# Two transformer layers on one core: the query projection put in place by DMAs instead of two masked products, and layer two's last 256 rows in one chunk instead of two

## The chip, the cores and the metric

One core of a Trainium2 chip runs the whole program: TensorE (PE, with its weight loads PEld), VectorE (DVE), ScalarE (ACT), GpSimd (POOL) and SyncE (SP, which here only issues DMAs), around an on-chip memory (SBUF) and the accumulators of TensorE (PSUM, eight banks of 128 partitions by 512 float32). The metric is device time in microseconds of one execution; the time of a kernel is the median of its runs.

## The reference, cut to what matters

The sequence has 2048 rows of 512 numbers in bfloat16. An attention layer A and a feed-forward layer B are applied twice, with the same weights both times. There are 32 heads of 16 numbers each, and the hidden width of B is 1792.

```python
def A(x, wqkv, wo):                       # 32 heads, 16 wide
    qkv = (x @ wqkv).reshape(B, S, 3, 32, 16).transpose(2, 0, 3, 1, 4)
    q, k, v = qkv
    p = softmax(einsum("bhqd,bhkd->bhqk", q, k) * 16 ** -0.5)
    return einsum("bhqk,bhkd->bhqd", p, v).transpose(0, 2, 1, 3).reshape(B, S, 512) @ wo
def Bff(x, w1, w2):
    return maximum(x @ w1, 0) @ w2
x = x + A(layernorm(x)); x = x + Bff(layernorm(x))
x = x + A(layernorm(x)); x = x + Bff(layernorm(x))
```

The exponentials are the mass of it: 2 layers x 32 heads x 2048 x 2048 = 268 million, in the kernel's layout 4096 blocks of 128 keys by 512 queries.

## The kernel before, in words

**Layout.** K and Q are kept transposed, 16 numbers of a head on 16 partitions. A *strip* T (there are four, T = 0 to 3) is 128 columns of the K or Q weights, so 128 partitions with eight heads; they sit as four row groups g of 32 partitions, each with two heads e = 0 and 1. A score matmul takes the 32 partitions of one group (line 1411); to keep the head e alone, the Q operand `qbuf[n % 2][:, e]` has zeros on the partitions of the other head. `q_masked` (line 680) makes both copies in one DVE instruction that reads the PSUM bank twice and multiplies it by a mask of 0 and the softmax scale: 128x1024 results.

**Runs and segments.** The queries are cut into chunks of rows, `chunks` (line 460): four of 512 rows in layer one (l = 0); in layer two (l = 1) two of 512, then three of 256 (lines 461 and 462), then two of 128 (lines 464 and 465); `LAST = 6` is the last chunk. A *run* is a layer, a chunk, a strip and a range of key blocks; its two *segments* are the heads e = 0 and 1 of the strip, and one segment's sums fill the one bank `ps_o`. Where a run takes only some of the key blocks (lines 862 to 871), its sums are *stored* in buffers of the layer that is not in use (`acc`, `acc0`, lines 145 to 151), and the later run adds them to its own: line 910 writes the sum of both to one of three buffers `u`.

**The loop** (line 1282) goes slot by slot, 1366 slots in all. A slot takes three blocks of scores (PSUM tiles `ps_s`, two of three banks each, used in turn). ACT exponentiates the three banks in one instruction of 128x1536 (line 1420), or only two of them, 128x1024, and the third goes to DVE, which makes the exponential of it with integer arithmetic and a cubic: line 1105 (`lin`) for each block, and for every two such blocks, a *pair*, lines 1146, 1157, 1146 and 1161 on 128x1024 (and line 1158 for the few pairs without prepared values). A block of DVE costs TensorE three products with V (`lin`, `step`, `cube`) instead of one.

**What sets the order.** The kernel writes out the order of every engine by hand: a planner keeps clocks for PE, DVE and ACT (`now_pe`, `now_dve`, `exp_end`) with costs for each instruction and lags for DMAs (line 80: `C_LAG`, `R_LAG`, `U_LAG`), and chooses what to issue next. Projections, output products and the feed-forward layer are *groups* of matmuls into the one bank `ps_f`, put between the slots (`mm_group`, line 428); each is evacuated by DVE. Line 1309 decides, by the DVE work already queued, whether a slot gives a block to DVE. An engine then executes in that order, each instruction waiting for its semaphores; so does the SP queue.

**Finishing a segment** (`finish_segment`, line 882): DVE copies `ps_o` to `u` (line 912; line 910 with stored sums), an SP DMA moves the row of sums to `c` (line 917), DVE takes the reciprocal (line 939), an SP DMA puts it back (line 940), a POOL DMA spreads it over 32 partitions into `r` (line 942; a `quick` segment uses a DVE shuffle, line 952), and DVE multiplies (line 928). Three sets of `u`, `r`, `c` go in turn; before the fourth is begun, the multiplication of the first is put into the order (lines 899 and 900).

**The start** (lines 182 to 201, 1172 to 1239): x and weights are loaded on the SP and ACT queues; K and Q weights 512 columns at a time (`load_w`, line 179); `w2`, 1.8 MB, is issued at line 195, then four slices of `w1` (line 719), then the transposes of the normalized rows of the next chunks (line 573), all on SP. POOL fills constants (lines 199 and 201) and has the small arithmetic of layernorm (lines 492 to 500). The normalized rows are in four buffers `xn` (line 157).

**The end** (from line 1454): after the last exponential, the last chunk's output product, layernorm, feed-forward layer and store, with lines 1473 (matmuls), 1483, 1513, 1525, 1527 and 1540; also one row block of the second part of the chunk before (`half_part`, line 1495).

Of the kernel before, what the change touches and what calls it, by code (L numbers as in the profile page):

```python
# [12 lines left out]
BF16 = mybir.dt.bfloat16  # L13
# [12 lines left out]
def kernel(  # L26
# [52 lines left out]
    FLOOR = 0.56  # L79
    C_LAG, R_LAG, U_LAG = 3600.0, 13000.0, 3000.0  # L80
    VLAG = 1
    X_ISSUE, X_LAG = 1400.0, 7500.0
    RSTD_LAG = 4000.0
    AHEAD = (8.0, 8.0)
    LATE = 0.0
# [22 lines left out]
    qmask = masks[:, 2:4]  # L108
    wqkv = sb([P, NDC, 3 * D], BF16, "wqkv")
    wo = sb([P, NDC, D], BF16, "wo")  # L110
# [67 lines left out]

    def load_w(engine, a):
        engine.dma_start(out=wqkv[:, :, a : a + D], in_=wq_src[:, :, a : a + D])  # L180

# [6 lines left out]
    nc.scalar.activation(out=warm[:], in_=warm[:], func=ACTF.Exp)  # L188
    load_w(nc.sync, D)
    load_w(nc.scalar, 0)  # L190
    load_x(nc.sync, (4, 5, 6, 7))
    load_w(nc.scalar, 2 * D)
    load_x(nc.sync, range(8, NTT))
    nc.sync.dma_start(out=wo[:], in_=A_wo[:, :].rearrange("(c p) f -> p c f", p=P))
    nc.sync.dma_start(out=w2[:], in_=B_w2[:, :].rearrange("(c p) f -> p c f", p=P))

    make_identity(nc, ident[:])
    for kb in range(NKB):
        nc.gpsimd.memset(vaug[0][kb][:, :, DH : DH + 2], 1.0)
    for kb in range(NKB - TPC):  # L200
        nc.gpsimd.memset(vaug[1][kb][:, :, DH : DH + 2], 1.0)


    wide = [True]
# [256 lines left out]
    HALF = TPC // 2  # L461
    for n in range(3):
        chunks[1, 2 + n] = (2 * TPC + n * HALF, HALF)
    chunks[1, 5] = (3 * TPC + HALF, 1)
    chunks[1, 6] = (3 * TPC + HALF + 1, 1)
    LAST = 6

# [46 lines left out]
    def ln_root(tag, rows):  # L514
# [11 lines left out]
        stt(out=y, in0=t1, scalar=1.5, in1=y, op0=ALU.add, op1=ALU.mult)  # L526

    def ln_apply(tag, tt, i):
        n = ln_n(tag)
        nc.vector.tensor_scalar(  # L530
            out=xnbuf[i][:], in0=x_t[tt][:],
            scalar1=mv[n][:, i, 0:1], scalar2=ya_[n][:, i : i + 1],
            op0=ALU.subtract, op1=ALU.mult,
        )

    def ln_transpose(tag, i, b=None, at_bank=None):
        pt = bank().bitcast(BF16) if b is None else b
        for c in range(NDC):
            ins = nc.tensor.transpose(
                pt[:, c * P : (c + 1) * P], xnbuf[i][:, c * P : (c + 1) * P], ident[:]  # L540
            )
            if wide[0]:
                uses(ins, in_bank[0] if b is None else at_bank)
        mark(("xT", tag, i), "pe")
        return pt[:, 0 : NDC * P].rearrange("p (c f) -> p c f", c=NDC)
# [4 lines left out]
    def ln_rows(tag, tt, n, i):  # L550
# [10 lines left out]
        if i == n - 1:  # L561

            def rstd():
                ln_seed(tag, n)
                mark(("rs", tag, 3), lag=RSTD_LAG)

            task(0, rstd, [("rs", tag, 3)], each(n, "st", tag) + old)
            def apply(k):
                ln_apply(tag, tt + k, k)
                if not by_dma(tag):  # L570
                    return
                _, l, j = tag
                nc.sync.dma_start_transpose(
                    out=xnT[j][:, :, k * P : (k + 1) * P], in_=xnbuf[k][:]
                )
                sp_free[0] = max(sp_free[0], now_dve[0]) + X_ISSUE
                lag = sp_free[0] + X_LAG - now_dve[0]
                mark(("xT", tag, k), lag=lag)
                mark(("xnT", tag, k), lag=lag)

            for k in range(n):
                task(
                    325, lambda k=k: apply(k),
                    [("xn", tag, k)] + [("xT", tag, k), ("xnT", tag, k)] * by_dma(tag),
                    [("xT", prev, k)] * (k < rows_of_prev) + [("rs", tag, 3)],
                )

    def ln_groups(tag, dst, at_column, n, war):
        groups = []
        for i in range(0, n, 2):  # L590
            hold = {}

            def piece(k, i=i, hold=hold):
                if not k % 2:
                    hold["b"] = bank()
                half = hold["b"].bitcast(BF16)[:, k % 2 * D : (k % 2 + 1) * D]
                ln_transpose(tag, k, half)
                m = min(2, n - i)
                if k - i < m - 1:
                    return  # L600
                pt = hold["b"].bitcast(BF16)[:, 0 : m * D].rearrange(
                    "p (i c f) -> p c i f", i=m, c=NDC
                )

                def fin():
                    a = at_column + i * P
                    nc.vector.tensor_copy(
                        out=dst[:, :, a : a + m * P].rearrange("p c (i f) -> p c i f", i=m), in_=pt
                    )
                    for of in range(i, k + 1):  # L610
                        mark(("xnT", tag, of))

                put_evac(609 if m == 2 else 342, fin)

            groups.append(
                group(
                    [(1.3, lambda k=k, piece=piece: piece(k)) for k in range(i, min(i + 2, n))],
                    [(key, tag, k) for key in ("xT", "xnT") for k in range(i, min(i + 2, n))],
                    [("xn", tag, k) for k in range(i, min(i + 2, n))] + war,
                )  # L620
# [6 lines left out]
    def k_mms(T, j):  # L627
        return [(wqkv[:, c, D + T * P : D + (T + 1) * P], xnT[j][:, c, :]) for c in range(NDC)]

# [10 lines left out]
    def v_mms(kb):  # L640
        j, i = divmod(kb, TPC)
        return [
            (xnT[j][:, c, i * P : (i + 1) * P], wqkv[:, c, 2 * D : 3 * D]) for c in range(NDC)
        ]
# [29 lines left out]
    def q_mms(l, j, T):  # L674
        xj, a, w = columns(l, j)
        return [
            (wqkv[:, c, T * P : (T + 1) * P], xnT[xj][:, c, a : a + w]) for c in range(NDC)
        ]
# [8 lines left out]
    def q_group(n, l, j, T):  # L687
        xj, _, w = columns(l, j)
        cost = 90 + 2.09 * w

        def fin(b):
            q_masked(n, b, w)
            mark(("q", n))

# [20 lines left out]
    def load_w1(n):  # L715

        if n < (NQS + LAST - 1) * NF + NW1:
            ft = n % NF
# [7 lines left out]

    def per_group(w):
        return min(QS // w, 2)

    def h_group(l, j, ft, war):  # L730
        n = (l * NQS + j) * NF + ft
        xj, a, w = columns(l, j)

        number = per_group(w)
        fts = range(ft, ft + number)
# [14 lines left out]
        def after():  # L750
            for f in range(number):
                load_w1(n + f + NW1)
            for _ in range(min(2, len(w1_to_load))):
                home, of = w1_to_load.popleft()
                mark(("kept", of), "pe", 6000.0)
                nc.sync.dma_start(
# [5 lines left out]
            [  # L762
                (
                    (w1_last[ft + f] if (l, j) == (1, LAST - 1) else w1buf[(n + f) % NW1])[:, c, :],
                    xnT[xj][:, c, a : a + w],
                )
                for f in range(number) for c in range(NDC)
            ],
            fin, made_here,
            each(w // P, "xnT", ("ln2", l, j)) + war + [  # L770
                ("kept", ft + f) if (l, j) == (1, LAST - 1) and ft + f >= NW1 else ("w1", n + f)
                for f in range(number)
            ],
            after=after, wide_by=w, sums=number, cost=77 + 1.045 * number * w,
        )

# [19 lines left out]
    def before(l, j):  # L796
# [3 lines left out]
        if not j:  # L800
            return 0, NQS - 1
        first, rows = chunks[l, j]
        return max(
            (l, b) for b in range(j)
            if chunks[l, b][0] % TPC <= first % TPC < chunks[l, b][0] % TPC + chunks[l, b][1]
        )
# [3 lines left out]
    def rest_of_chunk(l, j):  # L810

        if (l, j) == (1, LAST - 2):
            for ft in range(NF):
                home = (
                    w1buf[((l * NQS + LAST - 1) * NF + ft) % NW1] if ft < NW1
                    else (kt01 + kt2)[(ft - NW1) // 2][:, ft % 2, :].rearrange(
# [12 lines left out]
        )  # L829
        gs = [h_group(l, j, ft, war_h) for ft in range(0, NF, per_group(w))]  # L830
        gs += [z_group(l, j, i) for i in range((l, j) == (1, LAST - 1), n)]
# [47 lines left out]

    sums_wait = [0]  # L880

    def finish_segment(sg, last):
# [16 lines left out]
        if n >= NU:  # L899
            run_until(("m", n - NU))  # L900
        u, r, c = ubuf[n % NU], rbuf[n % NU], cbuf[n % NU]
        lane = DH if e == 0 else DH - 1
# [32 lines left out]
        ended[l, j] = ended.get((l, j), 0) + 1  # L935
        quick = ended[l, j] == NT or sg["load"] is not None and sg["busy"] or width == P

# [39 lines left out]
        elif sg is segs[-2]:  # L977
            task(1560 * width // P, direct_all, ots + [("m", n)], war + [("u", n)])
        else:
# [203 lines left out]
    for e in range(2):  # L1183
# [3 lines left out]
            op=ALU.add, axis=mybir.AxisListType.XY,  # L1187
        )
        nc.vector.tensor_scalar(
            out=qmask[:, e : e + 1], in0=mask[e], scalar1=SCALE * LOG2E * UNIT, scalar2=None,  # L1190
            op0=ALU.mult,
# [382 lines left out]
```

## Time and profile before

| what | value |
|---|---|
| time, median of 3 runs | 1583.8 us (1582.8 to 1585.81) |
| the profiled execution's own time | 1582.8 us |
| its span, first to last instruction | 1580.9 us |
| granted TensorE clock | 0.999 |
| first exponential begins | 14.98 us |
| last exponential ends | 1558.87 us |
| ACT busy with exponentials | 1539.8 us |
| matmul records of the scores (L1411) | 6699 |
| DMA moved | 44.98 MB, mean 28 GB/s |

The page gives, for each engine, the time in which it was busy, and the chain of work that ended last, followed back from the end. Groups of instructions are named by source line, engine, operation, and what they write and read. A group's mean duration reaches from start to end, and neighbouring instructions of one engine overlap a little, so that count times mean is over the busy time. The timeline gives start, duration, engine and line, and in brackets how long the engine had been idle and what released it. SPq is the SP queue's issuing of DMAs.

### The profile page before, as it was taken

The numbers are of one execution on the slowest core, as the hardware profiler recorded it, in microseconds if no ns is written. First come the engines' busy times: TensorE is split into PE (matmuls) and PEld (weight loads), VectorE is DVE, ScalarE is ACT, GpSimd is POOL, SyncE is SP. The second block draws the span as 40 slices with busy tenths as digits, with TensorE's granted clock in tenths as the row PEclk, the third lists the DMA queues.
The fourth block names the chain that finished last, engine by engine and source line by source line (L and its number), as shares of the span: only waits on it lengthen the run. The fifth ranks groups of instructions, "written<-read, shape, count | busy, mean of one in ns | idle before, by whom it ended". The sixth has DMA issues, their size and how long they took to land.

```text
span 1580.9 us, 48353 instructions
## 1 busy us (share of the span) xinstructions
PE 1431.2 (91%) x21308; PEld 551.6 (35%) x21311; DVE 1502.9 (95%) x2947; ACT 1549.1 (98%) x1387; POOL 96.6 (6%) x243
## 2 busy tenths in 40 slices
PE   8888889998999989999899998888999999999898
PEld 3222223232332222333223222222334444545665
DVE  7889999999999999999899999999999999999895
ACT  6999999999999999999999999999999999999995
POOL 2000001001010010000100000001001000010000
PEclk9999999999999999999999999999999999999999
DMA  6001100111012120120101000000210211212030
GB/s 194 15 2 24 21 9 16 42 29 24 6 19 43 25 29 7 22 52 12 26 2 27 22 2 1 2 4 9 59 21 17 43 34 27 60 25 59 18 75 16
DMA packets 130145, 44.98 MB, mean 28 GB/s; under 512 B 119280, under 2 KB 127216, under 8 KB 129936
## 3 DMA queue, kind: packets, MB, share of 16 engines
q1 hardware_dynamic: 116864, 29.37, 8.8%
q0 software_dynamic: 11728, 11.23, 4.0%
q8 instruction: 166, 2.72, 0.7%
q10 hardware_dynamic: 1344, 1.31, 0.3%
q14 instruction: 43, 0.35, 0.1%
HBM read 24.38 MB, written 2.10 MB: 17 GB/s over the span
## 4 chain that ended last, share of the span: by engine, by line
ACT 78%; PE 11%; DVE 8%; issue 2%; DMA 1%; SPq 0%; ACTq 0%; DVEq 0%
ACT e L1420 78%; PE ps_s L1411 4%; PE ps_f L446 3%; PE ps_o L998 3%; DVE lin L1105 2%; DVE step L1146 1%; DVE cube L1157 1%; DVE cube L1161 1%; PE ps_s L1473 1%; DVE ht L744 0%; DMA wqkv<-in_A_wqkv_dram 0%; DVE q L681 0%; DVE ot L928 0%; DMA w<-in_B_w_dram 0%; DVE u L912 0%
## 5 line engine op out<-in xcount | busy, mean ns | idle before, releaser
L1420 ACT ACTIVATE e<-ps_s 128x1024 bf16<-128x1024 f32 (+1 forms) x1366 | 1539.8, 1357 | 6.1 <-PE ps_s L1411 5.3
L1411 PE MATMUL ps_s<-q,ktp 32*128 32x512 bf16 (+2 forms) x6699 | 608.3, 324 | 112.8 <-ACT e L1420 102.1
L998 PE MATMUL ps_o<-e,vaug 128*32 128x512 bf16 (+2 forms) x4682 | 495.3, 328 | 8.4 <-DVE u L912 2.7
L1105 DVE TENSOR_SCALAR lin<-ps_s 128x512 int16<-128x512 f32 x696 | 475.9, 686 | 23.4 <-PE ps_s L1411 17.3
L1411 PEld LDWEIGHTS <-ktp 32*128 32x128 bf16 x6699 | 209.0, 91 | 560.6 <-issue 411.0
L998 PEld LDWEIGHTS <-vaug 128*32 128x32 bf16 x6644 | 175.8, 94 | 290.2 <-issue 265.3
L1146 DVE TENSOR_SCALAR step<-lin 128x1024 int16<-128x1024 int16 x696 | 274.2, 420 | 2.1 <-PE ps_o L998 1.2
L1157 DVE TENSOR_TENSOR cube<-step 128x1024 f16<-128x1024 bf16 x348 | 236.5, 684 | 1.7 <-PE ps_f L446 0.5
L1161 DVE TENSOR_TENSOR cube<-cube,lin 128x1024 bf16<-128x1024 f16 x348 | 236.6, 681 | 0.0
L998 PE MATMUL ps_o<-step,vaug 128*32 128x512 bf16 (+2 forms) x950 | 159.5, 327 | 0.0
L446 PE MATMUL ps_f<-w,ht 128*32 128x512 bf16 x1680 | 152.2, 381 | 1.2 <-DVE ht L744 0.5
L446 PE MATMUL ps_f<-xnT,w 128*32 128x512 bf16 (+2 forms) x2080 | 148.2, 341 | 4.9 <-DVE ht L744 3.1
L998 PE MATMUL ps_o<-cube,vthird 128*32 128x512 bf16 (+2 forms) x888 | 143.4, 326 | 0.0
L998 PE MATMUL ps_o<-lin,vaug 128*32 128x512 bf16 (+2 forms) x950 | 125.0, 326 | 6.2 <-DVE u L912 3.7
L446 PE MATMUL ps_f<-xnT,wqkv 128*32 128x512 bf16 (+2 forms) x1376 | 107.9, 351 | 5.2 <-DVE ht L744 1.1
L942 POOL DMA_DIRECT2D r<-u x53 | 39.0, 736 | 1077.6 <-DVE lin L1105 438.0
L446 PE MATMUL ps_f<-wo,ot 128*32 128x512 bf16 x992 | 88.0, 381 | 1.3 <-DVE x L705 1.0
L744 DVE TENSOR_SCALAR ht<-ps_f 128x512 bf16<-128x512 f32 (+1 forms) x107 | 73.0, 682 | 2.9 <-PE ps_f L446 2.3
L446 PEld LDWEIGHTS <-w 128*32 128x32 bf16 x2080 | 59.2, 96 | 34.6 <-issue 17.6
L681 DVE TENSOR_TENSOR q<-ps_f,masks 128x1024 bf16<-128x1024 f32 (+2 forms) x55 | 54.3, 987 | 7.8 <-PE ps_f L446 5.9
L446 PEld LDWEIGHTS <-ht 128*32 128x32 bf16 x1680 | 48.7, 96 | 28.7 <-issue 13.1
L998 PEld LDWEIGHTS <-vthird 128*32 128x32 bf16 x888 | 44.0, 95 | 28.5 <-issue 23.4
(106 smaller groups left out, 610.7 us busy)
## 6 DMA issues: line engine op xcount, KB each, us to landing
w<-in_B_w_dram SPq DMA_DIRECT2D x130, 128.0 KB
r<-u POOLq DMA_DIRECT2D x32, 256.0 KB, 7.4
r<-u POOLq DMA_DIRECT2D x21, 128.0 KB, 4.8
out_dram<-x SPq DMA_DIRECT2D x16, 128.0 KB
x<-in_A_x_dram SPq DMA_DIRECT2D x14, 128.0 KB
w<-in_B_w_dram SPq DMA_DIRECT2D x1, 1792.0 KB
ktp<-in_B_w_dram SPq DMA_DIRECT2D x10, 128.0 KB
wqkv<-in_A_wqkv_dram ACTq DMA_DIRECT2D x2, 512.0 KB
```

The source lines that it names most:

```text
L446: nc.tensor.matmul(out[cols], lhsT[:, cols], rhs, start=i % k == 0, stop=i % k == k - 1, tile_position=(0, 32 * g), skip_group_check=True,)
L681: return nc.vector.tensor_mul(out=qbuf[n % 2][:, :, 0:w], in0=b.rearrange("p (e q) -> p e q", e=1).to_broadcast((P, 2, w)), in1=qmask.rear ...
L744: nc.vector.tensor_scalar(out=out, in0=sums, scalar1=0.0, scalar2=None, op0=ALU.max)
L942: nc.gpsimd.dma_start(out=r[:, 0:width], in_=bass.AP(tensor=sums.tensor, offset=sums.offset, ap=[list(sums.ap[0]), [0, 32], [1, width]],),)
L998: nc.tensor.matmul(ps_o[32 * g : 32 * g + 32, 0 : sg["w"]], values[:, 4 * sg["T"] + g, 2 * e : 2 * e + 32], rhs, start=g not in sg["begun" ...
L1105: first = nc.vector.tensor_scalar(out=lin[which][:, half * QS : (half + 1) * QS], in0=src, scalar1=EXP_BIAS, scalar2=0.0, op0=ALU.add, op1 ...
L1146: nc.vector.tensor_scalar(out=stair, in0=line, scalar1=keep, scalar2=put, op0=ALU.bitwise_and, op1=ALU.bitwise_or,)
L1157: (609, lambda: nc.vector.tensor_mul(out=power, in0=mantissa, in1=mantissa)),
L1161: (609, lambda: nc.vector.tensor_mul(out=power.bitcast(BF16), in0=power, in1=line.bitcast(BF16))),
L1411: nc.tensor.matmul(b[:, a : a + sg["w"]], kt[32 * g : 32 * g + 32, kc : kc + P], qbuf[sg["n"] % 2][32 * g : 32 * g + 32, sg["e"], 0 : sg[" ...
L1420: ex = nc.scalar.activation(out=eb[:, 0 : place[m]], in_=b[:, 0 : place[m]], func=ACTF.Exp, scale=1.0 / (LOG2E * UNIT),)
L1473: uses(nc.tensor.matmul(out, lhsT, rhs, start=first, stop=last), b, needs=needs)
```

## The change

**Weights.** The K and Q weights get buffers of their own, `wkq`, in which the two heads of a group are interleaved: partition 2d + e of a group holds number d of head e. They are loaded strip by strip, 128 columns at a time, into the space of `w2` (`stage`) and copied to `wkq` by an engine: strip 0 by two ACT copies, strips 1 to 3 by six loads that POOL issues and six POOL copies. The load of `w2` therefore waits for these copies; in SP's order it stands ahead of the `w1` slices. POOL also clears `qbuf[1]` once. The V weights are a buffer `wv`.

**Q.** A Q group is read from PSUM once, by one DVE instruction into `xnbuf[3]` (128x512, scaled), and two SP DMAs copy the even partitions to the half e = 0 of `qbuf` and the odd ones to e = 1; the other partitions of each half stay zero. Where `xnbuf[3]` holds normalized rows that are still wanted, the masked product of before is used. The planner counts with 6 us for the DMAs.

**Sums.** A segment with stored sums adds `ps_o` to them in place, and goes on from that buffer instead of `u`; `u` and `r` come from one ring of six, and before a set `c` is used again only the reciprocal must have been put into the order. `R_LAG` is 10.5 instead of 13 us.

**Chunks.** Layer two's last 512 rows are two chunks of 256 (`LAST = 5`), not one of 256 and two of 128; what served the chunks of 128 goes (odd layernorm groups, two `w1` slices a step at line 753, `quick` for 128 columns). The end after the last exponential then has two row blocks instead of one.

```diff
-    C_LAG, R_LAG, U_LAG = 3600.0, 13000.0, 3000.0
+    C_LAG, R_LAG, U_LAG = 3600.0, 10500.0, 3000.0
+    Q_LAG = 6000.0
...
-    wqkv = sb([P, NDC, 3 * D], BF16, "wqkv")
+    wkq = sb([P, 2, 4, NDC, P], BF16, "wkq")
+    wv = sb([P, NDC, D], BF16, "wv")
...
+    def load_w(engine, k, T):
+        a = (1 - k) * D + T * P
+        engine.dma_start(out=stage[:, k, T], in_=wq_src[:, :, a : a + P])
+    def interleave(copy, k, T):
+        copy(
+            out=wkq[:, k, T].rearrange("p c (g d e) -> p (c g) e d", g=4, e=2),
+            in_=stage[:, k, T].rearrange("p c (g e d) -> p (c g) e d", g=4, e=2),
+        )
...
-    load_w(nc.sync, D)
-    load_w(nc.scalar, 0)
+    load_w(nc.sync, 0, 0)
+    load_w(nc.scalar, 1, 0)
...
+    for k in range(2):
+        interleave(nc.scalar.copy, k, 0)
...
-    nc.sync.dma_start(out=w2[:], in_=B_w2[:, :].rearrange("(c p) f -> p c f", p=P))
     make_identity(nc, ident[:])
+    nc.gpsimd.memset(qbuf[1][:], 0.0)
+    for T in range(1, 4):
+        for k in range(2):
+            load_w(nc.gpsimd, k, T)
...
+    for T in range(1, 4):
+        for k in range(2):
+            interleave(nc.gpsimd.tensor_copy, k, T)
+    nc.sync.dma_start(out=w2[:], in_=B_w2[:, :].rearrange("(c p) f -> p c f", p=P))
...
-    for n in range(3):
+    for n in range(4):
         chunks[1, 2 + n] = (2 * TPC + n * HALF, HALF)
-    chunks[1, 5] = (3 * TPC + HALF, 1)
-    chunks[1, 6] = (3 * TPC + HALF + 1, 1)
-    LAST = 6
+    LAST = 5
...
         def fin(b):
-            q_masked(n, b, w)
-            mark(("q", n))
+            if xn_waits[0]:
+                q_masked(n, b, w)
+                now_dve[0] += 13 + 1.045 * w
+                mark(("q", n))
+                return
+            qraw = xnbuf[TPC - 1]
+            nc.vector.tensor_scalar(
+                out=qraw[:, 0:w], in0=b, scalar1=SCALE * LOG2E * UNIT, scalar2=None, op0=ALU.mult
+            )
+            for e in range(2):
+                nc.sync.dma_start(out=qbuf[n % 2][e:P:2, e, 0:w], in_=qraw[e:P:2, 0:w])
+            mark(("q", n), lag=Q_LAG)
...
+    ring = deque((x, None) for us in zip(ubuf, rbuf) for x in us)
...
         if n >= NU:
-            run_until(("m", n - NU))
-        u, r, c = ubuf[n % NU], rbuf[n % NU], cbuf[n % NU]
+            run_until(("r", n - NU))
+        c = cbuf[n % NU]
+        def room():
+            buf, of = ring.popleft()
+            if of is not None:
+                run_until(("m", of))
+            ring.append((buf, n))
+            return buf
+        u = room() if sg["load"] is None else sg["load"]
+        r = room()
...
-        quick = ended[l, j] == NT or sg["load"] is not None and sg["busy"] or width == P
+        quick = ended[l, j] == NT or sg["load"] is not None and sg["busy"]
```

## The prediction

> **What bounds the kernel.** I read the engine shares first, then the chain that ended last, then the exponentials alone in windows of time, then the timelines of the two ends.
>
> ```profile
> PE 1431.2 (91%) x21308; PEld 551.6 (35%) x21311; DVE 1502.9 (95%) x2947; ACT 1549.1 (98%) x1387; POOL 96.6 (6%) x243
> ...
> ACT 78%; PE 11%; DVE 8%; issue 2%; DMA 1%; SPq 0%; ACTq 0%; DVEq 0%
> ```
>
> ACT sets the pace, DVE is nearly as full. The groups by shape give the prices:
>
> ```profile
> L1420 ACT ACTIVATE e<-ps_s 128x1536 bf16<-128x1536 f32 x669 | 1009.0, 1572 | 5.4 <-PE ps_s L1411 4.9 <-PE ps_o L998 0.3
> L1420 ACT ACTIVATE e<-ps_s 128x1024 bf16<-128x1024 f32 x696 | 751.3, 1152 | 0.7 <-PE ps_s L1411 0.4
> L1105 DVE TENSOR_SCALAR lin<-ps_s 128x512 int16<-128x512 f32 x696 | 475.9, 686 | 23.4 <-PE ps_s L1411 17.3
> ...
> L681 DVE TENSOR_TENSOR q<-ps_f,masks 128x1024 bf16<-128x1024 f32 x35 | 42.7, 1220 | 5.5 <-PE ps_f L446 5.4
> ```
>
> A block moved from ACT to DVE saves ACT 1572 - 1152 = 420 ns. The exponentials in windows (start:end, length, busy, count, clock, DMA share, GB/s):
>
> ```profile
> 15.00:100.00 85.00, 84.44 (x69) 1.00 0.20 50
> ...
> 1400.00:1500.00 100.00, 99.53 (x88) 1.00 0.17 34
> 1500.00:1540.00 40.00, 38.40 (x34) 1.00 0.38 81
> ```
>
> From the first exponential (14.98) to the end of the last (1558.87) pass 1543.9 us, of which 1539.8 are busy: only 4.1 us of idle can be won. So the time is start (15) + exponentials + their idle + the end (1580.9 - 1558.9 = 22.0), and I price each.
>
> **1. Exponentials: -6.7 us.** The order in which the changed program's instructions stand has 653 of 128x1536 and 712 of 128x1024 in place of 669 and 696: eight more pairs, 16 blocks fewer on ACT, 16 x 0.42 = 6.7. Does DVE have the room? A pair costs 2 x 686 + 2 x 420 (L1146) + 684 + 681 = 3.58 us, eight 28.6. Against that: 34 Q reads of 128x512 at the 0.69 of L1105 instead of 1.22 save 18.2; narrow Q (12 x 0.685 + 8 x 0.421 before, 16 x 0.421 after) saves 4.9; the finishing of 128-column segments (14 shuffles of 0.30, reciprocals, products, copies), less what six or seven more 256-column ones cost, and two sums saves about 11. Net -6: DVE stays at 95%, the freed time is spent on pairs. In-place sums keep their 20 additions of 0.68: no time, only buffers. Bounds -6.2 to -7.2.
>
> **2. The end: +4.9 us.** Timeline of before:
>
> ```profile
> 1555.54 3.33 ACT L1420 ACTIVATE e<-ps_s 128x1536 bf16<-128x1536 f32 x3
> ...
> 1559.54 0.30 DVE L959 STREAM_SHUFFLE r<-ps_o 128x128 f32<-128x128 f32 x1
> ...
> 1562.72 0.39 PE L1473 MATMUL ps_s<-x,ident 128*128 128x512 bf16 x1
> ...
> 1564.88 0.58 ACT L1483 CAST x<-ps_s 128x512 bf16<-128x512 f32 x1 [1.67 <-PE ps_s L1473]
> ...
> 1569.72 0.61 PE L1473 MATMUL ps_s<-xnT,w 128*128 128x128 bf16 x8 [0.46 <-ACT xnT L1513]
> ...
> 1577.45 0.58 ACT L1540 CAST x<-ps_s 128x512 bf16<-128x512 f32 x1 [0.53 <-PE ps_s L1473]
> ```
>
> With T the end of the last exponential, DVE has the sums at T+0.7 and the scaled output at T+2.3, but TensorE works off left-over hidden slices until T+3.8; the row is copied at T+6.0. After: no left-over slice stands behind the last score in the order, but two row blocks are due. TensorE: 18 matmuls of 0.216 (14 of them take 3.19 in this trace) end at T+4.7; DVE, with one more reciprocal and product (1.38) and a longer shuffle (0.15), ends at T+3.9, so TensorE is the later. Two copies and the first statistics: second statistics at T+5.75. From there 2.69 to the normalized row as before, 0.2 for a second aggregate, two rows 0.8, then 1.1 for transpose and copy: T+10.5 (before T+10.9). Hidden slices and sums: 14 times 4 matmuls of 256 columns (from rows of 128, 256 and 512 columns, 220, 272 and 382 ns: 0.43 ns a column) and 2 of 512, 0.87 each, 12.1, and some of the 1.6 us by which 7.7 exceeds such a count before; I take 12.8, T+23.3. Copy on DVE 0.69, second store 2.87 to the end as now: T+26.9. Bounds +3.5 (no such excess) and +6.2 (all of it, and DVE late with its last pair, whose chain of 6.9 us behind the copy of the second last sums stands over 7.4 us of exponentials).
>
> **3. The start: +1.5 us.** K of strip 1 lets the eleventh slot go; now Q of strip 1 comes by DMA too, behind w2 and four w1 slices on SP.
>
> ```profile
> 12.94 0.51 SPq L195 DMA_DIRECT2D w<-in_B_w_dram  x1
> 13.49 6.66 SPq L719 DMA_DIRECT2D w<-in_B_w_dram  x4
> ...
> 22.81 1.37 DVE L530 TENSOR_SCALAR xn<-x,mv,ya 128x512 bf16<-128x512 bf16 x4
> ...
> 27.53 0.68 DVE L631 CAST ktp<-ps_f 128x512 bf16<-128x512 f32 x1
> ```
>
> w2 must now wait for six POOL copies. No row shows these; POOL's 292 ns for 128x128 (less 0.1 for one element) gives 1.5 ns an element, 0.87 a copy; its memsets, 0.8 ns an element, 0.5. A DMA issue on POOL takes 0.68 to 1.18. POOL is done with ident at 1.4; clearing qbuf 0.9, six issues 4.1 to 7.1, the other memsets 1.8, six copies 3 to 5.2: 11 to 16 if the data are there, 21 if a 512-run issue costs twice 1.0. I take 14. SP then needs the 7.2 us that it needed (12.94 to 20.15), two Q issues of 0.55, and about 2.5 to land (the sums' way from issue at 166.0 to its reciprocal at 169.8 bounds that at 3.8): 24.8. **The wait that matters is on DVE:** the fourth normalized row goes to the buffer that Q is copied from, so it waits for both DMAs; it stood at 23.8 and comes at 23.3 with the cheaper Q. Behind it queue two V copies, statistics and the K copy of 27.53; PE and then ACT wait for that. 24.8 - 23.3 = 1.5. Bounds -0.3 (POOL done before 13) and +6 (POOL at 21, Q landing at 29.5). Strip 0 is no worse: 128 KB slices instead of 512 KB, and its two ACT copies of 0.59 have 6.3 us of idle ACT before 9.45.
>
> [...]
>
> **4. Idle in the middle: -1.0, and new waits +0.5.** 1500:1540 lost 1.6 us in the 128-column chunks, 1400:1500 with 256 columns 0.5 in 100; at that rate 1.0 goes (bounds 0 and -2.5). New: 100 Q issues of 0.55 on SP, whose queue mostly waits; the cover is that Q is asked for one run ahead. The shortest runs in the new order are 5 to 9 slots, 7 to 12 us, against 0.7 + 1.1 + 2.5. Without that cover each run would lose some 2 us. The spread sums are awaited after 10.5 instead of 13 us: reciprocal at 169.78, POOL's issue at 172.45, median landing 7.2 later, 9.9 in all; the longest landing 8.3 would make a late one 11, half a microsecond of DVE each. I take 0.5 (bounds 0 and +6).
>
> **Sum** -6.7 + 4.9 + 1.5 - 1.0 + 0.5 = -0.8: 1582.8 becomes 1582.0 for the profiled execution, which stood 1.0 below the median of the runs; so 1583.0 as median, against 1583.8.
>
> **Rivals.** *Faster:* POOL is done before 13, the end has no excess, and the idle of the middle goes: -6.7 + 3.5 - 0.3 - 2.0 = -5.5, 1578.3. For it: the end's excess over matmul counts may be latency that longer matmuls cover. Against: each term at its good end. *Slower, by the start:* POOL's issues or copies run to 21, w2 and with it Q come late, DVE stands at its fourth row until 29.5: +6 there, +3.7 in all, 1587.5. It decides from POOL ending at about 20. *Slower, by waits:* the shorter lag and the Q DMAs make DVE wait at half of the 59 spread sums: +6 to +8, 1590. *The change doesn't do what it says:* if Q's DMAs were late everywhere, the eight pairs would be paid for with idle ACT; that would look like the last.
>
> **Chances.** Forecast 0.46, faster 0.26, slower by the start 0.18, by waits 0.10. Within 0.2% (3.2 us, about what a measurement can tell from no change) is the forecast. Range: all good ends give 1577, all bad ones 1596; with 2 in 10 left out, 1577 to 1591; the forecast's own 1580.6 to 1587.
>
> **What would show it.** Exponentials busy 1533 +- 1; the end 26 to 28 us behind the last exponential; POOL's six copies done near 14 and the first transposes behind Q near 24; ACT idle under 2 us more before 40 us; about 34 Q evacuations of 0.69 and no DVE idle ahead of the products of the sums. Wrong, if ACT idles over 6 us between 15 and the last exponential.

## The result, and the profile after

The changed kernel takes 1622.3 us (median of 1620.62, 1621.02, 1623.57 and 1631.49) against 1583.68; the ratio is 1.0254, with a 95% interval of 1.0213 to 1.0294. It is slower by 2.5%, where no change was forecast (1583.0 us, 1577 to 1591). The profiled execution took 1620.62 us with a span of 1618.8, 37.9 more than the span of before. Ratios here are of undisturbed runs on one chip, so they can differ a little from the quotient of two medians.

The page of the changed kernel, engine totals and the chain that ended last (busy us, share of the span, instructions; then shares of the chain):

```profile
PE 1452.7 (90%) x19693; PEld 532.2 (33%) x19697; DVE 1503.5 (93%) x2942; ACT 1547.5 (96%) x1385; POOL 110.1 (7%) x253
...
ACT 66%; DVE 17%; PE 12%; DMA 2%; issue 2%; SPq 0%; DVEq 0%; ACTq 0%
```

ACT is still first, but its part of the chain fell from 78% to 66%: time passes in which it waits. With the first and last exponential (16.20 and 1590.20) and their busy time (1537.4) the 37.9 us can be put into the four terms of the prediction:

| term | forecast | measured in the profiled execution |
|---|---|---|
| exponentials, busy | -6.7 | -2.4 (653 and 712 of them, as forecast) |
| start: first exponential, and idle to 60 us | +1.5 | +1.2 and +1.9 |
| idle from 60 to 1500 us (2.0 before) | +0.5 | +32.3 |
| idle behind 1500 | -1.0 | -1.7 |
| end: last exponential to the last instruction | +4.9 | +6.6 (28.6 in place of 22.0) |

So one term holds almost all of it. The exponentials of the changed kernel in windows of time (start:end, length, busy and count, granted clock, DMA share, GB/s):

```profile
15.00:60.00 45.00, 41.50 (x33) 1.00 0.43 107
...
75.00:95.00 20.00, 15.41 (x14) 0.74 0.04 14
...
455.00:485.00 30.00, 26.23 (x24) 0.89 0.07 15
1015.00:1085.00 70.00, 61.18 (x52) 0.83 0.05 12
1165.00:1205.00 40.00, 29.12 (x26) 0.87 0.16 33
```

The last four windows lack 4.6, 3.8, 8.8 and 10.9 us; before, the same windows lacked 0.5 in all, at a clock of 1.00. Where exponentials are missing, the clock is low too. The table of waits names what is new there (who waited for whom; us in total, times, longest):

```profile
PE ps_s L1451 <- DMA q<-xn: 14.2, 7, 6.3
...
DVE xn L555 <- DMA q<-xn: 5.7, 5, 2.9
```

TensorE waited seven times for a Q that came by DMA; the waits end at 78.72, 1022.55, 1038.65, 1053.86, 1068.41, 1175.55 and 1196.34 us. Here is the second, from the timeline of the changed kernel (start us, us, engine, line, what; in brackets the idle time before it and its releaser):

```profile
1020.04 0.68 DVE L722 TENSOR_SCALAR xn<-ps_f 128x512 bf16<-128x512 f32 x1
...
1020.75 1.10 SPq L726 DMA_DIRECT2D q<-xn  x2
1021.40 0.39 PE L1451 MATMUL ps_s<-q,ktp 32*128 32x512 bf16 x2 [0.40 <-ACT e L1460]
1022.55 0.59 PE L1451 MATMUL ps_s<-q,ktp 32*128 32x512 bf16 x4 [0.77 <-DMA q<-xn]
...
1023.18 0.69 DVE L1140 TENSOR_SCALAR lin<-ps_s 128x512 int16<-128x512 f32 x1 [2.45 <-PE ps_s L1451]
1023.18 3.54 ACT L1460 ACTIVATE e<-ps_s 128x1024 bf16<-128x1024 f32 x3 [0.49 <-PE ps_s L1451]
```

DVE reads Q from PSUM, SP issues the two DMAs, and 1.8 us after the first issue TensorE can go on. Two of the slot's three blocks had been scored at 1021.4; the third, the one that needed the new Q, is the block that DVE takes (`lin`), and ACT's exponential of the other two starts only with it. TensorE in the changed kernel by single microseconds around this place (the third and fourth numbers are its busy time and the granted clock):

```profile
1020.00:1021.00 1.00, 0.94 (x10) 1.00 0.00 0
1021.00:1022.00 1.00, 0.39 (x2) 1.00 0.09 33
1022.00:1023.00 1.00, 0.45 (x4) 1.00 0.30 98
...
1024.00:1025.00 1.00, 1.00 (x9) 0.50 0.00 0
1029.00:1030.00 1.00, 1.00 (x11) 0.50 0.00 0
...
1031.00:1032.00 1.00, 1.00 (x9) 1.00 0.00 0
```

A wait of 0.77 us is followed by 6.83 us at half clock (1023.75 to 1030.58 in the trace's record of the clock), in which TensorE is busy all the time and ACT still idles half a microsecond ahead of two of the five exponentials that begin in it. The whole program has eleven such spells, 65 us in all, each of some 3.4 us or twice or three times that; eight of them begin in or within 2.2 us behind one of the seven waits for Q or the longest wait of DVE. The kernel before has one, at 112.41 us.

### The profile page after: what moved, and what is told of

Its sections match the earlier page's. It is cut to its first block, busy times and chain, and to the rows that moved or that the text cites. A ratio compares the mean times of both kernels' runs of the same rounds, so it can differ in the third digit from the quotient of the medians.

```text
span 1618.8 us, 45352 instructions
## 1 busy us (share of the span) xinstructions
PE 1452.7 (90%) x19693; PEld 532.2 (33%) x19697; DVE 1503.5 (93%) x2942; ACT 1547.5 (96%) x1385; POOL 110.1 (7%) x253
## 4 chain that ended last, share of the span: by engine, by line
ACT 66%; DVE 17%; PE 12%; DMA 2%; issue 2%; SPq 0%; DVEq 0%; ACTq 0%
ACT e L1460 66%; PE ps_s L1451 4%; DVE lin L1140 4%; PE ps_o L1033 4%; PE ps_f L470 3%; DVE step L1181 2%; DVE cube L1192 2%; DVE cube L1196 2%; DMA q<-xn 2%; PE ps_s L1513 1%; DVE ht L775 1%; DVE stats L505 1%; DVE xn L722 1%; DVE xn L555 0%; DVE ot L963 0%
## 5 line engine op out<-in xcount | busy, mean ns | idle before, releaser
L1460 ACT ACTIVATE e<-ps_s 128x1024 bf16<-128x1024 f32 (+1 forms) x1366 | 1537.4, 1345 | 38.6 <-PE ps_s L1451 34.9
L1451 PE MATMUL ps_s<-q,ktp 32*128 32x512 bf16 (+1 forms) x6061 | 614.2, 346 | 117.3 <-ACT e L1460 93.5
L1033 PE MATMUL ps_o<-e,vaug 128*32 128x512 bf16 (+1 forms) x4226 | 507.1, 349 | 11.6 <-DVE u L947 6.9
L1451 PEld LDWEIGHTS <-ktp 32*128 32x128 bf16 x6061 | 193.1, 92 | 577.4 <-issue 432.6
L1033 PE MATMUL ps_o<-step,vaug 128*32 128x512 bf16 (+1 forms) x894 | 160.5, 345 | 1.1 <-DVE step L1181 1.1
L470 PE MATMUL ps_f<-xnT,w 128*32 128x512 bf16 (+1 forms) x2016 | 152.4, 347 | 5.6 <-DVE ht L775 3.4
L1033 PE MATMUL ps_o<-cube,vthird 128*32 128x512 bf16 (+1 forms) x846 | 150.4, 339 | 2.1 <-DVE cube L1196 2.1
L1033 PE MATMUL ps_o<-lin,vaug 128*32 128x512 bf16 (+1 forms) x894 | 130.4, 342 | 6.9 <-DVE u L947 5.1
L470 PE MATMUL ps_f<-xnT,wkq 128*32 128x512 bf16 (+1 forms) x1312 | 109.6, 369 | 6.0 <-DVE vaug L691 2.1
L775 DVE TENSOR_SCALAR ht<-ps_f 128x512 bf16<-128x512 f32 x105 | 72.1, 687 | 3.5 <-PE ps_f L470 3.0
L470 PE MATMUL ps_f<-wv,xnT 128*32 128x512 bf16 x496 | 45.5, 395 | 4.8 <-DVE vaug L691 2.9
```

The source lines that it names most:

```text
L470: nc.tensor.matmul(out[cols], lhsT[:, cols], rhs, start=i % k == 0, stop=i % k == k - 1, tile_position=(0, 32 * g), skip_group_check=True,)
L775: nc.vector.tensor_scalar(out=out, in0=sums, scalar1=0.0, scalar2=None, op0=ALU.max)
L1033: nc.tensor.matmul(ps_o[32 * g : 32 * g + 32, 0 : sg["w"]], values[:, 4 * sg["T"] + g, 2 * e : 2 * e + 32], rhs, start=g not in sg["begun" ...
L1451: nc.tensor.matmul(b[:, a : a + sg["w"]], kt[32 * g : 32 * g + 32, kc : kc + P], qbuf[sg["n"] % 2][32 * g : 32 * g + 32, sg["e"], 0 : sg[" ...
L1460: ex = nc.scalar.activation(out=eb[:, 0 : place[m]], in_=b[:, 0 : place[m]], func=ACTF.Exp, scale=1.0 / (LOG2E * UNIT),)
```

## The experiments

**Theory A:** the idle time is waits for the Q DMAs, and the low clock that they bring. **Rival B:** the 256-row chunk, the in-place sums with the shorter lag, or the start make it.

**e1_masked: no Q DMA at all.**

```diff
-            if xn_waits[0]:
+            if True:
                 q_masked(n, b, w)
```

> The changed kernel, but every Q is put in place by DVE's two masked products from PSUM (1.22 us a strip), as before; no Q DMA is issued. Chunks, in-place sums and the interleaved weights stay. Theory A (late Q DMAs, and the half clock that follows each wait, are the whole of the idle time): ACT's idle ahead of the exponentials falls from 38.6 to about 6 us; the program has 665 of 128x1536 and 700 of 128x1024, 4 blocks fewer than before, -1.7; the start costs 1.2, the end 5 to 6.6: 1588 us (1585 to 1592). Rival B (the 256-row chunk, the in-place sums or the shorter lag make the idle): 1610 or more.

Measured: ratio 1.0032 (1.0019 to 1.0045), 1588.8 us on the base of 1583.7. ACT's idle ahead of the exponentials is 7.2 us, the clock 0.997. Rival B is out: without the Q DMAs the rest of the change costs 5 us, not 38.

**e2_select: Q by DMA only where it is early.**

```diff
-            if xn_waits[0]:
+            till = next((k for k, x in enumerate(units) if any(y[0]["n"] == n for y in x)), 99)
+            if xn_waits[0] or till < SOON * W or any(
+                k[0] == "xn" and k[2] == TPC - 1 for t in dve_q for k in t["makes"]
+            ):
                 q_masked(n, b, w)
```

> The changed kernel, but Q goes by DMA only where its first use is 27 or more blocks (nine slots) ahead and the last normalized row is not about to be written; elsewhere by masked products. 32 of 51 strips still go by DMA. Theory A: no PE wait for Q over 0.5 us, clock 1.00 from 1000 to 1200, idle near 6 us; exponentials 659 and 706 (10 blocks fewer than before, -4.2), start +1.2, end +5 to 6.6: 1585.5 us (1582 to 1589). Rival B: over 1600. Rival C (queueing on SP's ring also hits Qs asked early): PE still waits at one or two of the 256-column strips, 6 us each: 1592 to 1598.

Measured: ratio 1.0017 (1.0005 to 1.0029), 1586.4 us; no wait of PE for a Q DMA shows, idle 7.9 us, clock 0.998. With 32 Qs by DMA it is no slower than with none: the operation itself is not the loss, only its being late.

**e3_busy: the same waits, but TensorE has something to do.** Q comes as late as in the changed kernel; the added matmuls write the bank that the scores overwrite.

```diff
+    FRESH = {5: 8, 29: 4, 30: 6, 31: 5, 32: 3, 35: 11, 36: 29}
...
+                if sg["n"] in fresh and times_no == 0:
+                    for _ in range(fresh.pop(sg["n"])):
+                        nc.tensor.matmul(
+                            b[:, a : a + sg["w"]], ident[:], wo[:, 0, 0 : sg["w"]],
+                            start=True, stop=True,
+                        )
```

> The changed kernel with TensorE kept busy while it waits for Q: ahead of the first score of the seven strips whose Q came late, 3 to 29 matmuls of 512 columns on ready operands (the measured wait divided by 0.216), into the bank that the scores then overwrite. Q comes no earlier. Theory A1 (the wait itself is the smaller half; the half clock after it is the larger): the granted clock stays 1.00 at 76 to 90, 1020 to 1080 and 1175 to 1200 us, and some 10 us go (8 to 13): 1611 us (1608 to 1614). Theory A2 (the wait alone counts): 1621 +- 2.

Measured: ratio 1.0133 (1.0116 to 1.0151) where the changed kernel has 1.0254 (1.0213 to 1.0294): 13 us are gone by the medians, 19 by the ratios (with both intervals 12 to 26), though Q is no earlier. A2 (1621) is out; A1 forecast 8 to 13, so the half clock weighs at least as much as it said. The exponentials of e3_busy in the window of the four short runs:

```profile
1015.00:1085.00 70.00, 66.59 (x58) 1.00 0.05 13
```

The clock is 1.00 and 3.4 us are missing instead of 8.8: here 3.4 us are the waits, 5.4 the half clock behind them. At 75 to 95 it was 1.8 instead of 4.6; at 1165 to 1205, where one wait lasts 6.3 us, 10.2 instead of 10.9. These windows give 9 us. The profiled execution was the slowest of the four (1616.03) and lost 7.3 us from 15 to 60, 3.8 more than the changed kernel's, with half clock from 28.24 to 38.48; so the windows and the medians do not have to meet.

**e4_chunk: the kernel before, with only the last 256 rows in one chunk.** What follows from these lines in the change goes with them.

```diff
-    for n in range(3):
+    for n in range(4):
         chunks[1, 2 + n] = (2 * TPC + n * HALF, HALF)
-    chunks[1, 5] = (3 * TPC + HALF, 1)
-    chunks[1, 6] = (3 * TPC + HALF + 1, 1)
-    LAST = 6
+    LAST = 5
```

> The kernel before, with only the last 256 rows as one chunk; masked Q, plain weights, sums not in place. Exponentials 663 and 702 (6 blocks fewer, -2.5). If the end is the term that I mis-sized by two (+6.6 in place of +4.9): 1583.7 - 2.5 - 1.0 (idle of the middle) + 6 = 1586 us (1584 to 1589). If the clock holds at the end here: 1584.5. If the chunk itself makes idle time (rival B): over 1595.

Measured: ratio 1.0000 (0.9991 to 1.001). Its busy exponentials are 1.2 us less than before (663 and 702), its end 28.0 us, with half clock from 1557.92 to 1561.34, its first exponential 0.7 us earlier, which the change does not touch. It was expected 2 us higher; the chunk is no loss and no gain.

**e5_early: Q made in the slot in which it is asked for.** 
```diff
                 if n < len(runs):
                     urgent.append(q_group(n, *runs[n]))
+                    run_until(("q", n))
```

> The changed kernel, all Qs but the first by DMA, but Q of the next run is made at once when it is asked for (its products and its read from PSUM are forced into the slot in which the run before begins) instead of when the planner finds room, up to six slots later. 651 and 714 exponentials. Theory A' (what failed is the lead: one run ahead was when Q was asked for, not when it was made): no PE wait for Q in the four short runs near 1020 to 1080 us; the clock stays 1.00 there; the waits of DVE's fourth normalized row stay, 5 of 6 us in all: 1583.7 + start 1.2 + end 5 to 6.6 - exponentials 7.7 + idle for the DVE waits 5 to 10 = 1590 us (1585 to 1598). Rival (DVE runs so late against the plan that any DMA'd Q of a run of some ten slots is late): 1605 or more, PE waiting for Q over 6 us.

Measured: ratio 1.1749 (1.171 to 1.1789). The edit changes the computation: it puts the next run's Q into the buffer of the run before, whose last blocks are scored later in that slot, and it forces all that Q is made from out of its place (by the code). ACT idles 263 us. This run is inconclusive: it says nothing of the lead.

Which instruction reads the late Q gave another theory. In all seven places the slot that waits gives a block to DVE. **Theory A'':** the planner draws that block from the *next* run, whose own first blocks come later; it asks only that Q has been read from PSUM, and not that the DMA has landed.

**e9_land: a pair takes a later run's blocks only when Q should have landed.**

```diff
-                            and at([("q", sg["n"])], "pe") is not None
+                            and (at([("q", sg["n"])], "pe") or 1e9) <= now_pe[0] + SLACK
```

> The changed kernel, all but two Qs by DMA as in it; the one edit: a pair (the blocks that DVE takes) may be drawn from a later run only when the planned landing of that run's Q has passed, not as soon as Q has been read from PSUM. Theory A'' (in all seven places the first reader of a late Q is a pair that the planner drew from the next run in the slot after Q was read; the run's own first blocks come five to ten slots later): no PE wait for Q of over 0.5 us and no half clock at 76 to 90, 1020 to 1080 and 1175 to 1200 us. The pairs that reached ahead are lost too: 669 and 696 exponentials, as in the kernel before. So 1583.7 + 0 + start 1 + end 5 to 6.6 + idle for DVE's waits at the fourth normalized row 5 to 8 = 1596 us (1592 to 1601). Rival A' (the runs' own lead is too short): PE still waits in the four short runs, 1605 or more.

Measured: ratio 1.0088 (1.006 to 1.0117), 1597.6 us. No wait of PE for a Q DMA shows, with all Qs but two still by DMA. The exponentials of e9_land:

```profile
75.00:95.00 20.00, 20.00 (x17) 1.00 0.04 15
...
1015.00:1085.00 70.00, 70.00 (x60) 1.00 0.05 11
1165.00:1205.00 40.00, 40.00 (x36) 1.00 0.12 28
```

Nothing is missing in any of the three. A'' holds, and A' (the runs' own lead) is out. The price shows too: 669 and 696 exponentials, so with this rule none of the eight pairs that the change had won is left. The profiled execution's span is still 15.9 us over the kernel before: 6.6 at the end, with a spell of half clock in it, 5.9 of idle time (DVE still waits 3.1 us for Q DMAs), 2.5 at the start and 0.9 of exponentials.

**e10_rows: masked products where the Q DMA would hold up DVE's fourth normalized row,** the last three lines of e2_select's condition alone.

> The changed kernel, with masked products for a Q that is read from PSUM while DVE still has the last normalized row of a chunk to write; all other Qs by DMA, pairs reach ahead as in the changed kernel. It takes away DVE's waits for a Q DMA ahead of that row (5.7 us in five places, 2.9 at 466), and so the half clock at 470. 659 and 706 exponentials. If those waits cost what the windows at 255 to 285 and 455 to 485 show (2.0 and 3.8) and one or two more: -5 to -8 against the changed kernel, +2.5 for six pairs fewer: 1618 us (1613 to 1622). Rival (they cost nothing, DVE's waits are hidden): 1623 to 1626.

Measured: ratio 1.0152 (1.0129 to 1.0174), 1607.8 us, better than expected (1613 to 1622). The waits of DVE are gone, nothing is missing at 455 to 485, and from the first exponential to 60 us 0.4 us are idle instead of 2.3. At 255 to 285, which the expectation counted to these waits, 2.1 us are still missing; no wait of DVE for a Q DMA stands there in the changed kernel either. And the plan shifted also: TensorE's waits for Q fell from 14.2 to 9.3 us, and the last late Q waits 2.66 us instead of 6.32. So the 3.8 and 1.9 us of the two windows are what goes with the DVE waits; what more of the 15 is theirs isn't told apart.

**e6_actq and e11_quick: why one Q took 7.3 us.** For six of the late Qs the score that waits begins 1.8 to 3.1 us behind the first issue, for the seventh (256 columns) 7.3. In e6_actq two Qs go out on ACT's queue:

```diff
-                nc.sync.dma_start(out=qbuf[n % 2][e:P:2, e, 0:w], in_=qraw[e:P:2, 0:w])
+                queue = nc.scalar if n in (35, 36) else nc.sync
+                queue.dma_start(out=qbuf[n % 2][e:P:2, e, 0:w], in_=qraw[e:P:2, 0:w])
```

> The changed kernel, with the DMAs of the two Qs near 1172 and 1189 us (3.1 and 7.3 us from issue to the score that waits) issued from ACT's queue instead of SP's. Theory R (they stand behind weight slices in SP's ring): the second lands some 2 us after its issue. Theory P (they share the transfer engines with the 256 KB spread of sums that POOL issued at 1188.0, which lands at about the same time): it still takes 5 us or more. The time is not the point; ACT's issues may cost it a few us.

Measured: issued at 1191.64 on ACT's queue, score at 1198.96, again 7.3 us. So it was not the weights in SP's queue that held it up. In e11_quick one segment's sums are spread by DVE, so that POOL's DMA at 1188.0 falls away:

```diff
-        quick = ended[l, j] == NT or sg["load"] is not None and sg["busy"]
+        quick = ended[l, j] == NT or sg["load"] is not None and sg["busy"] or (sg["n"], e) == (33, 1)
```

> The changed kernel, with the sums of one segment spread by DVE's shuffle instead of by the 256 KB DMA that POOL issued at 1188.0 (its queue and SP's hold one issue less; one later narrow Q is masked, as the plan falls). Theory P (the Q of 1189, 7.3 us from issue to the waiting score on SP's queue and on ACT's, shared the transfer engines with that spread): it lands in 2 to 3.5 us, PE's wait of 6.3 us falls to 1 to 2.5, the time by some 4 to 6 us. Rival (narrow Qs, 512 bytes a partition row, are slow in themselves): it stays at 6 us or more.

The changed kernel's issue and the score that waits:

```profile
1189.06 2.85 SPq L726 DMA_DIRECT2D q<-xn  x2
...
1196.34 0.58 PE L1451 MATMUL ps_s<-q,ktp 32*128 32x256 bf16 x2 [6.32 <-DMA q<-xn]
```

and the same two in e11_quick:

```profile
1187.97 1.46 SPq L726 DMA_DIRECT2D q<-xn  x2
...
1190.13 0.37 PE L1451 MATMUL ps_s<-q,ktp 32*128 32x256 bf16 x2 [1.19 <-DMA q<-xn]
```

Without the 256 KB spread beside it the Q lands in 2.2 us and the issue itself takes 1.46 instead of 2.85. Theory P holds as far as the spread is what delays the Q. That the two share the DMA engines is not shown to be the way: from 1190 to 1196 us the 16 engines were busy only 0.16 to 0.32 of the time, and a packet of Q took 28 ns beside the spread and 27 without it; the 128 packets came over 5.8 us instead of 1.2. (One execution; its span is 1608.6, 10 less, of which the window 1165 to 1205 gives 6.2.)

**e7_pool: POOL's copies held until DVE has written four rows.** On top of e2_select; the six copies and the load of `w2` move behind one line that reads the fourth row.

```diff
     for i in range(TPC):
         ln_apply(tag, i, i)
         mark(("xn", tag, i))
+    nc.gpsimd.tensor_copy(out=warm[:], in_=xnbuf[TPC - 1][:, 0:1])
+    for T in range(1, 4):
+        for k in range(2):
+            interleave(nc.gpsimd.tensor_copy, k, T)
```

> The kernel of e2_select, with POOL's six interleaving copies held until DVE has written the first four normalized rows (POOL reads one element of the fourth row ahead of them). Theory (POOL's copies stop DVE while they run: one of the four rows took 1.84 us in the changed kernel, 1.19 in e2_select, and 0.41 in the kernel before, where POOL copies nothing): all four rows take 0.40 to 0.45, the first exponential starts at 15.0 or before instead of 15.9 to 16.2. Rival (the long row is a matter of the data or of the DMAs): a row stays over 0.6 us, the first exponential at 15.7 or later. The two waits for strips 1 to 3 of the weights may come later by 1 us, which the second transposes can show.

DVE's first four normalized rows in the changed kernel (shortest, median and longest ns) and in e7_pool:

```profile
L555 DVE TENSOR_SCALAR xn<-x,mv,ya x4: 395/404/1840, 8.3 to 10.7; 128x512 bf16<-128x512 bf16 x4
```

```profile
L552 DVE TENSOR_SCALAR xn<-x,mv,ya x4: 394/402/851, 8.0 to 9.4; 128x512 bf16<-128x512 bf16 x4
```

The first exponential starts at 14.83 instead of 15.86 (e2_select), in one execution each (1585.86 us here). One row still takes 0.85, with POOL's constants beside it, so the bound of 0.6 in the expectation was missed for that row; the 1.84 is gone with the copies.

**e8_qonly and e12_noring: the parts that paid, put together.** e8_qonly is the kernel before with Q as in e2_select and POOL held, without the chunk and the in-place sums; e12_noring is e2_select with POOL held, without the in-place sums, so both have these lines of the kernel before:

```diff
-    C_LAG, R_LAG, U_LAG = 3600.0, 10500.0, 3000.0
+    C_LAG, R_LAG, U_LAG = 3600.0, 13000.0, 3000.0
...
-            run_until(("r", n - NU))
...
-        u = room() if sg["load"] is None else sg["load"]
-        r = room()
+            run_until(("m", n - NU))
+        u, r, c = ubuf[n % NU], rbuf[n % NU], cbuf[n % NU]
```

> The kernel before with the part of the change that paid: interleaved Q and K weights, Q by DMA where its first use is nine slots ahead (as in e2_select), POOL's copies held as in e7_pool; the last 256 rows stay in two chunks of 128, and the stored sums are not finished in place. 663 and 702 exponentials in place of 669 and 696 of before: 6 x 0.42 = -2.5; end 22.0 as before, start 0 to +1: 1582 us, ratio 0.9987 (0.998 to 1.0005). Rival (Q DMAs cost idle time even where they are early, or the pairs bought cost DVE as much): ratio over 1.001.

> The changed kernel without the sums finished in place (and with the lag of before), Q by DMA only where it is early (as in e2_select), POOL's copies held (as in e7_pool). 657 and 708 exponentials, 12 blocks fewer than before: -5.0; end 26.9 against 22.0: +4.9; start 0; waits +1: 1584.6 us, ratio 1.0005 (0.999 to 1.002). If the in-place sums are worth something beyond buffers it stands above e2_select (1.0017).

Measured: 1.0004 (0.9987 to 1.0022) and 0.9998 (0.9985 to 1.0011). Neither can be told from the kernel before. In e12_noring the busy exponentials fall by 5.7 us (657 and 708), the end costs 4.8, the start 0.3, and idle time 2.5. One late Q is left in each: TensorE waits 1.6 us for it till 1328.11 and 1.3 till 1326.83, and half clock follows (from 1328.82 and 1328.10). No version here beats the kernel before by what a measurement can tell.

## Why the prediction was wrong, point by point

**The step that failed** is in part 4: "the cover is that Q is asked for one run ahead. The shortest runs in the new order are 5 to 9 slots, 7 to 12 us, against 0.7 + 1.1 + 2.5." The second number, an estimate, was fair: 0.7 to read and 1.8 to 3.1 from issue to score, but for one Q with 7.3. The first was the wrong quantity. It measured from run to run; what counts is from Q's read to its *first reader* in TensorE's order, and that reader was a pair drawn ahead, due 1.5 us behind the start of the read at 1171.73 (1175.55 - 2.36) and 1.7 behind that at 1020.04. The planner keeps the lag of the DMA (`Q_LAG`), but the choice of a pair asks whether Q is made, not when. With masked products the two were the same, which is why the kernel before never paid. e9_land shows it: with no Q late in TensorE's order, and all but two Qs by DMA, the ratio falls from 1.0254 to 1.0088. The term "new waits +0.5" measured +32.3, and the sign that the prediction named for being wrong, over 6 us of idle ACT, came with 36.6. The prediction had the order of TensorE's instructions and could have read each run's first score from it.

**"Without that cover each run would lose some 2 us"** was near for a wait, but not for its cost. Seven waits are 14.2 us of TensorE's idle time; with DVE's five (5.7) and the half clock they made nearly all of the 32.3 us by which ACT's idle time grew (e1_masked, without Q DMAs, has 2.6 of them). The prediction had no term for the clock, since the profile of before shows 1.00 in nearly every window. e3_busy sizes it: 9 us in its windows, 13 to 19 by the times, of 38.

*The half clock.* The changed kernel's eleven spells of half clock last 3.41 us (four), 6.83 (six) and 10.24 (one): one, two or three times 3.41. In the 3.41 us ahead of the fall at 1023.75 TensorE was busy 0.66 of the time, ahead of those at 1040.82 and 470.79 0.49 and 0.39.

In each of the traces all spells begin on one grid of steps of 3.41 us, and whether the clock falls goes with how busy TensorE was in the step just ended. Of the steps at full clock between the first and the last exponential, in the traces of all kernels here but e5_early, half clock followed 30 of 33 in which TensorE was busy less than 0.60 of the time, 28 of 61 at 0.60 to 0.67, 7 of 222 at 0.67 to 0.75, and 3 of 5486 above. By these counts a wait of 0.77 us alone, 0.23 of a step, would seldom do it; the step ahead of 1023.75 had other gaps too, and near 0.65 the same share was followed by half clock in one place and not in another.

**Exponentials, -6.7: the count was right, the time -2.4.** An exponential alone takes 1.02 us (128x1024), one in a row 1.152 - 0.23 = 0.92, since neighbours overlap by some 0.23 us (314 us of overlap at 1365 junctions before). At 39 gaps, 0.1 each, 3.9 of the missing 4.3 us are lost this way; that is worked out, not tried. Where the gaps are few the term held: -3.8 in e2_select (forecast by the same price -4.2), -5.7 in e12_noring (-5.0), less well -1.2 in e4_chunk and -1.8 in e8_qonly (-2.5 each).

**The end, +4.9: right as a sum where the clock is whole.** It is 26.6 us in e1_masked, 26.9 in e2_select, 26.8 in e12_noring (forecast 26.9). In the changed kernel it is 28.6. The other traces agree: 26.5 and 27.0 without a spell of half clock in it (e11_quick, e3_busy), 28.0 to 29.4 with one (e4_chunk, e6_actq, e7_pool, e9_land, e10_rows). The first output products of the last chunk there, and in e1_masked:

```profile
1591.10 3.00 PE L1513 MATMUL ps_s<-wo,ot 128*128 128x512 bf16 x7 [0.33 <-issue]
```

```profile
1559.54 1.67 PE L1513 MATMUL ps_s<-wo,ot 128*128 128x512 bf16 x7 [0.16 <-issue]
```

Seven matmuls take 3.00 us instead of 1.67; the clock is half from 1590.36 to 1593.78. The terms inside it were off both ways: DVE's part ended at T+3.7 (forecast 3.9), TensorE's at T+6.1 (4.7).

**The start, +1.5: right in size for the wrong reason.** POOL was done at 14.4 (forecast 14) and the fourth row behind Q's DMA came at 26.14, later than forecast (24.8). What moved the first exponential by 1.2 us stood in no term: DVE's first normalized row began at 8.34 and ended at 10.18, and POOL's first two copies ran from 8.60 to 10.03. DVE's four rows before, and DVE and POOL after:

```profile
8.09 1.38 DVE L530 TENSOR_SCALAR xn<-x,mv,ya 128x512 bf16<-128x512 bf16 x4
```

```profile
8.34 2.81 DVE L555 TENSOR_SCALAR xn<-x,mv,ya 128x512 bf16<-128x512 bf16 x4
...
8.60 1.43 POOL L191 COPY wkq<-w 128x512 bf16<-128x512 bf16 x2
```

In each of the seven other traces with POOL's copies at this place one or two of the four rows take 0.83 to 1.84 us too; without them none takes over 0.41, but for a first one of up to 0.85 beside POOL's constants (e7_pool, e8_qonly, e12_noring). The 1.2 us is one execution's: the first exponential of these seven begins at 15.2 to 20.2, the two latest (17.5 in e9_land, 20.2 in e11_quick) with half clock ahead of it. The prediction priced POOL's copies by POOL's time alone and called strip 0 "no worse". In e7_pool, which is e2_select with the copies held, the longest row takes 0.85 instead of 1.19; by what way POOL's work holds up a DVE instruction no run shows. Q of strip 1 was issued at 22.28, with the weights still moving (214 GB/s from 22 to 24 us), and the row behind it began 3.9 us later; no run shows whether Q stood behind the weights. For the one Q of 7.3 us e6_actq shows that SP's queue was not the cause: from ACT's it took 7.3 too.

**Idle behind 1500, -1.0:** -1.7, right. **The shorter lag, bounds 0 to +6:** no cost shows; the products of the sums wait 0.2 us for the spread. The in-place sums gave nothing either: e12_noring, without them and with the lag of before, is no slower than e2_select.

**The rivals.** "The change doesn't do what it says" named late Q DMAs, though everywhere and not at seven of 50, and gave them the time of "slower, by waits", +6 to +8 and 1590; it had the right kind of wait and a fifth of its price.

## What to carry to other kernels

When a value that an engine wrote directly is to come by DMA, find its first reader in the order of the reading engine, not the place where it is asked for; every test in a hand-written schedule that asks "made?" has to ask "landed?". Even so the DMAs gave no gain here: the ratio is 1.0088 with that test, 1.0017 with the old way where Q would be late. Here a wait of TensorE cost more than itself where the work around it kept it less than full (from 1015 to 1085 us 3.4 us of waits and 5.4 of half clock): add the low clock behind it to the price, and fill the wait if it can't be removed. Copies on POOL at a place where DVE is on the path have to be priced on DVE too (a row of 0.41 us took 1.84 beside them).

## What the runs showed of the hardware

A wait of 0.77 us was followed by 6.83 us at half clock, with TensorE busy 0.66 of the 3.41 us before; at 0.60 to 0.67 half clock followed 28 of 61 such steps, under 0.60 30 of 33, above 0.75 3 of 5486. From the issue of two transfers of 32 KB within SBUF to the score that waited for them it was 2.2 us in e11_quick, without a 256 KB DMA of POOL beside them, and 7.3 with it, on SP's queue (the changed kernel) and on ACT's (e6_actq) alike; the issue took 2.85 us (SP) and 2.98 (ACT) instead of 1.46. A DVE instruction that took 0.41 us in the kernel before took 1.84 in the changed kernel while POOL copied.
